# A replaced table of order keys, an earlier bias row, and five weight subtractions moved to GpSimd, in a fused attention and mixture-of-experts kernel

## The chip, the cores and the metric

One core of a Trainium2 chip. The metric is the device time of one execution in microseconds (us). The engines are called as in the profile: PE is TensorE (matmuls; PEld its weight loads), DVE is VectorE, ACT is ScalarE, POOL is GpSimd, SP is the engine that issues most DMAs.

## What is computed

```python
# attention: q, k, v (4, 8, 576, 64), s (4, 8, 576)
scores = (1 / sqrt(D)) * np.matmul(q, k.transpose(0, 1, 3, 2))
cum = np.cumsum(np.maximum(s, 0.0), axis=-1)
bias = -(cum[:, :, :, None] - cum[:, :, None, :])
scores = np.where(causal, -1000000000.0, scores + np.minimum(bias, 0.0))
scores = scores - np.max(scores, axis=-1, keepdims=True)
attn = np.exp(scores)
attn = attn / (np.sum(attn, axis=-1, keepdims=True) + 1e-09)
x = np.matmul(attn, v)                      # as 2304 tokens of 512
# first mixture: w1, w2, w3 (512, 768), w_out (768, 512)
h = np.maximum(np.maximum(x @ w1, x @ w2), x @ w3)
x = h @ w_out
# second: 8 experts, one per token
logits = x @ w_gate + modality_bias[modality_id]
e_idx = np.argmax(logits, axis=1)
gate_w = softmax(logits)[np.arange(N), e_idx]
h = np.maximum(x[mask] @ w1[e], 0.0)        # for each expert e, mask = e_idx == e
out[mask] = gate_w[mask, None] * (h @ w2[e])
```

## The kernel before

Attention runs in 16 pairs of heads (32 heads, h = 0 to 31). To keep float32 precision at the matmul's reduced format, operands are split into a rounded high part and a low part (value minus high). Per head, `load_x` brings q and k (L358, L359), `load_k` the two bias rows that are appended to k (L373 for the first pair, from a scratch tile; L375 for the others, from a copy in memory that `rows_out`, L379, writes in two transfers). `k_high` and `q_high` (L387, L390, mostly ACT) round, `k_again` (L393, POOL) rounds k once more beside the bias rows, `k_low` and `q_low` (L397, L400, POOL) subtract. `scores` makes a bank of scores with two matmuls, L407 (high by high) and L408 (low parts and bias rows). Six banks make one causal head, of 288, 448, 288, 320, 192 and 64 columns. On DVE `least` (L416) masks a bank and takes the row's extreme, on ACT `expo` (L423) exponentiates and sums. PE transposes the result (`turn`, L428), DVE or ACT copies it out (`turned`, L433), and once for each pair `values_of` (L463) multiplies with v in 24 matmuls. The sums go through L437 (ACT), L440 (DVE), L444 (PE), L448 (ACT) and two DMAs to be multiplied in at L469 and L473 (DVE).

Between attention's work PE does **fills**: matmuls of the first mixture on batches whose attention is done. `fill` does three matmuls of 128x288 (L249 high by high, L250 and L251 with a low part); 12 matmuls fill a bank, which ACT copies (L502) or DVE folds in by a maximum (L504). `fx_high` (L487, ACT) and `fx_low` (L491, POOL) split the tokens. The same lines L249 to L251 with 128x384 are the rest of the first mixture, after attention.

The weights arrive as float64 and are **converted** in steps on a 128x512 piece: load (L213, SP, 0.5 MB), L225 (ACT), L227, L229, L231 (DVE), a rounding (L234, a DMA by POOL, for nine early pieces; L236, ACT, for fifteen later ones), and the subtraction for the low part, L238 (POOL for the early ones, DVE for the later).

What sets the order: in attention, every step is a `Job` with an engine, an estimated duration, predecessors and a key. `planned` (L117 on) is a list scheduler: on the engine whose next job can start first it takes, among those that can start within 60 ns, the one with the lowest key. A key is the head's number times `KEY["T"]` plus the entry of table `KEY` (L94) for that kind of step. The jobs are then written out in that order and keep it. Behind them come the later conversions (`convert_rest`, L847), 15 in all, six of which are asked for (`LEAD`) before the first projection, and the rest of both mixtures; their order is set by the framework's own scheduler.

Of the kernel before, what the change touches and what calls it, by code (L numbers as in the profile page):

```python
# [5 lines left out]
F32 = mybir.dt.float32  # L6
# [3 lines left out]
ALU = mybir.AluOpType  # L10
# [6 lines left out]
T = B * S  # L17
# [44 lines left out]
LEAD = 6  # L62
# [28 lines left out]
CONV = [(0, 3), (1, 3), (2, 5), (3, 7), (4, 7), (5, 9), (6, 13), (7, 15), (8, 17)]  # L91
W_READY, SET_H = 15000, 24
WIRE_FROM, WIRE_TO, WIRE_SLOW = 1300, 900, 1.0
KEY = {"s3": 262888, "T": 15750, "wl": 29386, "wz": 48740, "w1": 225687, "wd": 68498, "ws": 411529, "lx": 95995, "lv": 209700, "ck": 138477, "kb": -116340, "kl": -53033, "ql": -58361, "s": 115494, "mn": -5610, "ex": 153024, "ds": 361, "t": 18694, "dt": 19213, "cp": -53151, "r1": -208485, "r2": -212716, "rt": 15596, "rc": -242689, "rw": 44183, "pv": -165391, "x": -56845, "xc": 100720, "xs": -74110, "fe": -88191}  # L94
R_MOE1 = (2, 4, 7)
R_MOE2 = (1, 3, 5)

# [84 lines left out]
def fused_kernel(tc, qk, vd, sd, w64, mod, wg, wgt, mb, we, cst, csi, out):  # L182
    nc = tc.nc
    V, A, G, P, SP = nc.vector, nc.scalar, nc.gpsimd, nc.tensor, nc.sync
    top = ExitStack()
    with top:
# [33 lines left out]
        def converted(f, k, pool, tag, raw, early):  # L220
            h = pool.tile([128, 512], F32R, tag=tag, name="w_h")
            lo = pool.tile([128, 512], F32R, tag=tag, name="w_l")
            z = zsp.tile([128, 512], F32, name="w_z")
            zi = z.bitcast(I32)
            A.activation(out=z, in_=raw.bitcast(F32)[:, :, 1], func=ACTF.Abs, scale=2.0 ** -112)  # L225
            yield
            V.tensor_scalar(out=zi, in0=zi, scalar1=3, scalar2=None, op0=ALU.logical_shift_left)  # L227
            yield
            V.scalar_tensor_tensor(out=zi, in0=raw[:, :, 0], scalar=29, in1=zi, op0=ALU.logical_shift_right, op1=ALU.bitwise_or)  # L229
            yield  # L230
            V.scalar_tensor_tensor(out=zi, in0=raw[:, :, 1], scalar=-2 ** 31, in1=zi, op0=ALU.bitwise_and, op1=ALU.bitwise_or)  # L231
            yield
            if early and W_DMA:
                G.dma_start(out=h, in_=z)  # L234
            else:
                A.copy(out=h, in_=z)  # L236
            yield
            (G if early else V).tensor_tensor(out=lo, in0=z, in1=h.bitcast(F32), op=ALU.subtract)  # L238
            W[f][0][k] = h
            W[f][1][k] = lo  # L240

# [18 lines left out]
        with ExitStack() as es:  # L260

            s3 = xbp.tile([32, 3, S], F32, tag="xb", name="s3")
# [83 lines left out]
            def job(name, run, eng, ns, key, **k):  # L346
                j = Job(run, eng, ns, key, **k)
                jobs.append(j)
                st[name] = j
                return j  # L350

            def at(h, what, n=0):
                return h * KEY["T"] + KEY[what] + n

            def load_x(h):
                p, j = divmod(h, 2)
                x = tl["x", h] = qkp.tile([128, 2, S], F32, name="qk_r", bufs=QR_BUFS)
                SP.dma_start(out=x[64:128, 1], in_=qk[PORD[p], 64:128, 1, j])  # L358
                (SP if h else A).dma_start(out=x[:, 0], in_=qk[PORD[p], :, 0, j])  # L359
                if h == 0:  # L360
                    SP.dma_start(out=mask[:, S - 128:S], in_=cst[:, 256:384])
                    SP.dma_start(out=ident, in_=cst[:, 0:128])

            def k_tile(h):
                if ("k_b", h) not in tl:
                    tl["k_b", h] = qkp.tile([66, S], F32R, name="k_b", bufs=KB_BUFS)
                return tl["k_b", h]

            def load_k(h):
                p, j = divmod(h, 2)  # L370
                k_b = k_tile(h)
                if p == 0:
                    SP.dma_start(out=k_b.bitcast(F32)[64:66], in_=augk.bitcast(F32)[16 * j + PORD[0]:16 * j + PORD[0] + 1])  # L373
                else:
                    SP.dma_start(out=k_b.bitcast(F32)[64:66], in_=dk[PORD[p], :, j])  # L375
# [5 lines left out]
            def values_in(p):  # L381
                v_r = tl["v_r", p] = vp.tile([128, 5, 128], F32, name="v_r")
                SP.dma_start(out=v_r, in_=vd[PORD[p]])

            def k_high(h):
                hl = tl["hl", h] = qkp.tile([128, 2, S], F32R, name="hl", bufs=HL_BUFS)
                (G.tensor_copy if h in CK_POOL else A.copy)(out=hl[64:128, 0], in_=tl["x", h][64:128, 1])  # L387
# [4 lines left out]
            def k_again(h):  # L392
                G.tensor_copy(out=k_tile(h)[0:64], in_=tl["x", h][64:128, 1])  # L393

            def k_low(h):
                hl = tl["hl", h]
                (V if h in KL_DVE else G).tensor_tensor(out=hl[0:64, 0], in0=tl["x", h][64:128, 1], in1=hl.bitcast(F32)[64:128, 0], op=ALU.subtract)  # L397

            def q_low(h):
                G.tensor_tensor(out=qbs[h % QB_N][0:64], in0=tl["x", h][0:64, 0], in1=tl["hl", h].bitcast(F32)[0:64, 1], op=ALU.subtract)  # L400
# [17 lines left out]
            def expo(h, c):  # L418
                p, j = divmod(h, 2)
                if ("l", p) not in tl:  # L420
                    tl["l", p] = ss.tile([128, 2, 5], F32, name="l")
                ec = e_bufs[h % E_N][:, EOFF[c]:EOFF[c] + QC[c][2]]
                A.activation(out=ec, in_=ec, func=ACTF.Exp, bias=tl["mn", h][:, c:c + 1], scale=-1.0, accum_out=tl["l", p][:, j, c:c + 1])  # L423
# [54 lines left out]
            def w_step(n, k):  # L478
                if k == 0:
                    tl["conv", n] = converted(*tl["raw", n])  # L480
                next(tl["conv", n], None)
# [27 lines left out]
            for n, h in CONV:  # L509
                raw, z = Slot("raw"), Slot("z")  # L510
# [4 lines left out]
            sums_s = a = job("s2", s_sums, "DVE", 1346, -1e9, after=[a])  # L515
            b = job("s3", s_high, "ACT", 575, KEY["s3"], after=[a], ready=4350)
            a = job("s4", s_from, "DVE", 360, -1e9, after=[a], lock=True)
            s_low_ = job("s5", s_low, "DVE", 750, -1e9, after=[a, b], lock=True)
            rows = job("rows", rows_out, "SP", 1300, -1e8, after=[s_low_], wire=300)
            turns, highs = None, []  # L520
            for h in range(2 * NP):
                p, j = divmod(h, 2)
                s_x, s_k, s_h, s_q, s_e = (Slot(n) for n in ("qk", "kb", "hl", "qb", "e"))
                lx = job(("lx", h), lambda h=h: load_x(h), "SP", 1900 if h == 0 else 1130, at(h, "lx") if h > 2 else -1e9 + h, takes=[s_x], ready=750, wire=1700)
                if j == 0:
                    s_v, s_p, done = Slot("vr"), [], []
                    lv = job(("lv", p), lambda p=p: values_in(p), "SP", 430, at(h, "lv") if p else -9e8, takes=[s_v], wire=1300, ready=2000)
                ck = job(("ck", h), lambda h=h: k_high(h), "POOL" if h in CK_POOL else "ACT", 671 if h in CK_POOL else 640, at(h, "ck"), after=[lx], takes=[s_h], uses=[s_x], ready=4350)
                cq = job(("cq", h), lambda h=h: q_high(h), "ACT", 600, at(h, "ck", 1), after=[lx, ck], uses=[s_x, s_h])
                if h > 1:  # L530
                    lk = job(("lk", h), lambda h=h: load_k(h), "SP", 300 if h > 1 else 450, at(h, "lx", 1) if h > 1 else -2e8 + h, after=[rows], takes=[s_k], wire=100)
                kb = job(("kb", h), lambda h=h: k_again(h), "POOL", 657, at(h, "kb"), after=[lx, lk] if h > 1 else [lx], takes=[s_k] if h < 2 else [], uses=[s_x, s_k])
                if h < 2:
                    lk = job(("lk", h), lambda h=h: load_k(h), "SP", 300 if h > 1 else 450, at(h, "lx", 1) if h > 1 else -2e8 + h, after=[kb, s_low_], uses=[s_k], wire=100)
                kl = job(("kl", h), lambda h=h: k_low(h), "DVE" if h in KL_DVE else "POOL", 850 if h in KL_DVE else 1415, at(h, "kl"), after=[ck], uses=[s_x, s_h], lock=h in KL_DVE, tail=10 if h in KL_DVE else 0)
                ql = job(("ql", h), lambda h=h: q_low(h), "POOL", 1410, at(h, "ql"), after=[cq], takes=[s_q], uses=[s_x, s_h])
                ex = {}
                for n, (c, k) in enumerate(C_ORDER):
# [3 lines left out]
                    if k or c < 4:  # L542
                        ex[c] = job(("ex", h, c), lambda h=h, c=c: expo(h, c), "ACT", EXP_NS[c], at(h, "ex", n * KEY["ds"]), after=[a], uses=[s_e], tail=0)
                done += ex.values()
# [298 lines left out]
        rest = [(f, k) for f in range(NPRE, NF1) for k in range(3)] + [(f, 3) for f in range(NF1)]  # L843

        N_REST = len(rest)
# [9 lines left out]
        early = []  # L855
        late = []
        for w in range(NW):
# [25 lines left out]
            for i in range(MW // 128):  # L883
                t = w * (MW // 128) + i
# [82 lines left out]
        at = unp.tile([128, U + 1], F32, name="at")  # L967
# [98 lines left out]
```

## Time and profile before

| | before |
|---|---|
| runs, lowest / median / highest | 733.42 / 734.62 / 736.40 us |
| the profiled execution | 734.0 us |
| its span, first to last instruction | 732.2 us |
| busy, share of the span: PE / DVE / ACT / POOL | 97% / 68% / 55% / 31% |
| DMA, mean over the span | 142 GB/s |
| granted TensorE clock, mean | 0.999 |

The span is the time from the first to the last instruction; the execution's own time has 1.8 us more around it. A share of busy time is an average over stages with different limits, so the stretches are looked at one by one below.

### The profile page before, as it was taken

Reading aid. Unit: us, or ns where it says so; the run is one execution under the profiler, and the core shown is the slowest. Engines: PE = TensorE matmul, PEld = TensorE weight load, DVE = VectorE, ACT = ScalarE, POOL = GpSimd, SP = SyncE. Lnnn points to the kernel's source line nnn. Section 1 sums busy time; section 2 is a strip of 40 time slices with the busy share of each in tenths; the row PEclk is TensorE's granted clock in tenths of the full one; section 3 lists DMA queues with packets and bytes.
Section 4 is the critical chain, followed back from the end, with each engine's and each line's share of the span. In section 5 each row is a group of like instructions: output and inputs, shape, how many; then the busy total and the mean of one; then the engine's idle time right before and its main releaser. Section 6 shows DMA issues by size and latency. Waiting matters only on the chain. (4 is left out here: it accounts for less than half of the span.)

```text
span 732.2 us, 13634 instructions
## 1 busy us (share of the span) xinstructions
PE 708.2 (97%) x4602; PEld 633.5 (87%) x4602; DVE 497.4 (68%) x1542; ACT 399.9 (55%) x984; POOL 225.3 (31%) x235
## 2 busy tenths in 40 slices
PE   4899999999999999999999999999999999999996
PEld 3677788878899899899999898999889988999884
DVE  5999787978667932673959796747775665565640
ACT  6899989898644511222222322636564765566631
POOL 8789868776101300010010101041421222212101
PEclk9999999999999999999999999999999999999999
DMA  7476666655236400101001101767567666666600
GB/s 214 144 219 188 203 184 212 190 151 147 81 127 209 164 26 6 49 1 31 36 23 54 52 21 51 258 159 247 153 214 265 225 208 220 212 224 226 222 35 19
DMA packets 43535, 103.83 MB, mean 142 GB/s; under 512 B 9472, under 2 KB 13472, under 8 KB 43456
## 3 DMA queue, kind: packets, MB, share of 16 engines
q1 hardware_dynamic: 35808, 86.04, 37.6%
q0 software_dynamic: 4912, 11.82, 5.1%
q10 hardware_dynamic: 2736, 5.01, 1.9%
q8 instruction: 38, 0.62, 0.4%
q14 instruction: 41, 0.34, 0.2%
HBM read 88.83 MB, written 12.18 MB: 138 GB/s over the span
## 5 line engine op out<-in xcount | busy, mean ns | idle before, releaser
L249 PE MATMUL a_ps<-xh,w_h 128*128 128x384 f32 (+2 forms) x492 | 159.4, 325 | 1.9 <-DVE h L504 1.1
L251 PE MATMUL a_ps<-xh,w_l 128*128 128x384 f32 (+2 forms) x492 | 155.8, 318 | 0.0
L250 PE MATMUL a_ps<-xl,w_h 128*128 128x384 f32 (+2 forms) x492 | 155.7, 317 | 0.0
L768 DVE TENSOR_TENSOR e_l<-e_raw,e_h 128x512 fp32r<-128x512 f32 x160 | 103.9, 689 | 13.5 <-ACT e_h L767 12.1
L767 ACT CAST e_h<-e_raw 128x512 fp32r<-128x512 f32 x160 | 92.9, 622 | 15.9 <-DMA e_raw<-in_we 6.9
L249 PEld LDWEIGHTS a_ps<-xh,w_h 128*128 128x128 f32 x492 | 92.6, 188 | 3.8 <-DVE h L504 1.4
L423 ACT ACTIVATE e<-e,mn 128x448 f32<-128x448 f32 (+4 forms) x160 | 88.6, 557 | 8.5 <-DVE mn L416 8.1
L250 PEld LDWEIGHTS a_ps<-xl,w_h 128*128 128x128 f32 x492 | 92.7, 188 | 0.3
L676 POOL DMA_INDIRECT table<-meta,si x18 | 19.6, 1088 | 238.1 <-DVE nm L664 83.2
L251 PEld LDWEIGHTS a_ps<-xh,w_l 128*128 128x128 f32 x492 | 92.4, 188 | 0.1
L798 PE MATMUL h_ps<-x2t,e_h 128*128 128x256 f32 x288 | 81.0, 282 | 0.0
L799 PE MATMUL h_ps<-x2t,e_l 128*128 128x256 f32 x288 | 80.9, 282 | 0.0
L797 PE MATMUL h_ps<-x2t,e_h 128*128 128x256 f32 x288 | 80.5, 282 | 0.0
L651 DVE CUSTOM_DVE_ANT_0 junk<-x,wg 128x512 bf16<-128x512 f32 x96 | 65.8, 686 | 17.2 <-ACT x L729 16.3
L407 PE MATMUL s_ps<-hl 128*128 128x288 f32 (+1 forms) x192 | 66.0, 354 | 9.9 <-DVE hl L397 6.9
L428 PE MATMUL t_ps<-ident,e 128*128 128x128 f32 x480 | 70.1, 280 | 1.4 <-DVE pt L433 0.6
L416 DVE CUSTOM_DVE_ANT_0 e<-s_ps,mask 128x288 f32<-128x288 f32 (+4 forms) x160 | 63.4, 424 | 9.5 <-PE s_ps L408 9.1
L827 PE MATMUL y_ps<-e_h,gh 128*128 128x512 f32 x152 | 61.5, 405 | 0.4 <-ACT gh L819 0.4
L408 PE MATMUL s_ps<-k_b,q_b 66*128 66x288 f32 (+1 forms) x192 | 57.9, 317 | 4.1 <-DMA k_b<-augk 3.9
L428 PEld LDWEIGHTS t_ps<-ident,e 128*128 128x128 f32 x480 | 56.0, 143 | 5.7 <-DVE pt L433 2.0
L829 PE MATMUL y_ps<-e_h,gl 128*128 128x512 f32 x152 | 60.7, 400 | 0.0
L828 PE MATMUL y_ps<-e_l,gh 128*128 128x512 f32 x152 | 60.0, 395 | 0.0
(179 smaller groups left out, 1484.0 us busy)
## 6 DMA issues: line engine op xcount, KB each, us to landing
e_raw<-in_we SPq DMA_DIRECT2D x80, 512.0 KB
w_raw<-in_w SPq DMA_DIRECT2D x24, 512.0 KB
qk_r<-in_qk SPq DMA_DIRECT2D x31, 288.0 KB
v_r<-in_vd SPq DMA_DIRECT2D x16, 320.0 KB
rb<-r_d SPq DMA_DIRECT2D x32, 160.0 KB
qk_r<-in_qk SPq DMA_DIRECT2D x32, 144.0 KB
x2d<-x ACTq DMA_DIRECT2D x18, 256.0 KB
w_h<-w_z POOLq DMA_DIRECT2D x9, 256.0 KB, 3.9
```

The source lines that it names most:

```text
L249: P.matmul(a_ps, wh[:, c], xh, start=c == 0, stop=False)
L250: P.matmul(a_ps, wh[:, c], xl, start=False, stop=False)
L251: P.matmul(a_ps, wl[:, c], xh, start=False, stop=c == 3)
L407: P.matmul(s_ps, hl[:, 1, q0:q0 + 128], hl[:, 0, k0:k0 + n], start=True, stop=False)
L423: A.activation(out=ec, in_=ec, func=ACTF.Exp, bias=tl["mn", h][:, c:c + 1], scale=-1.0, accum_out=tl["l", p][:, j, c:c + 1])
L428: P.transpose(out=t_ps[:, n * 128:(n + 1) * 128], in_=e_bufs[h % E_N][:, EOFF[c] + kb * 128:EOFF[c] + (kb + 1) * 128], identity=ident)
L651: V.tensor_tensor_reduce(out=junk, in0=x2, in1=wg_sb[ei // 2][:, ei % 2, :], scale=1.0, scalar=0.0, op0=ALU.mult, op1=ALU.add, accum_out=l ...
L767: A.copy(out=h, in_=raw[:, a])
L768: V.tensor_tensor(out=lo, in0=raw[:, a], in1=h.bitcast(F32), op=ALU.subtract)
L797: P.matmul(h_ps, w(hs, f, c), xt[:, 0, c], start=c == 0, stop=False)
L798: P.matmul(h_ps, w(hs, f, c), xt[:, 1, c], start=False, stop=False)
L799: P.matmul(h_ps, w(ls, f, c), xt[:, 0, c], start=False, stop=c == 3)
```

## The change

Three edits. The table of keys is replaced by another, so that the whole order of the attention part changes. The planner is told that the write of the bias rows (`rows`) can't start before 8.5 us of its own clock, and that the first two heads' bias rows take 0.7 us longer to land. And of the 15 later conversions, the first five subtract on POOL instead of DVE. No instruction is added or taken away.

```diff
-KEY = {"s3": 262888, "T": 15750, "wl": 29386, "wz": 48740, "w1": 225687, "wd": 68498, "ws": 411529, "lx": 95995, "lv": 209700, "ck": 138477, "kb": -116340, "kl": -53033, "ql": -58361, "s": 115494, "mn": -5610, "ex": 153024, "ds": 361, "t": 18694, "dt": 19213, "cp": -53151, "r1": -208485, "r2": -212716, "rt": 15596, "rc": -242689, "rw": 44183, "pv": -165391, "x": -56845, "xc": 100720, "xs": -74110, "fe": -88191}
+KEY = {"s3": -97664, "T": 7000, "wl": 40053, "wz": -18589, "w1": 32737, "wd": -43995, "ws": 98173, "lx": -66595, "lv": -5637, "ck": -4681, "kb": -52279, "kl": 21128, "ql": 9680, "s": -4267, "mn": -4185, "ex": 13414, "ds": 50, "t": 10767, "dt": 50, "cp": -42063, "r1": -6337, "r2": -61094, "rt": -71579, "rc": 7287, "rw": -3704, "pv": -70498, "x": -40039, "xc": 39659, "xs": -51512, "fe": 6144}
...
-            (G if early else V).tensor_tensor(out=lo, in0=z, in1=h.bitcast(F32), op=ALU.subtract)
+            (G if early or len(rest) > N_REST - LEAD else V).tensor_tensor(out=lo, in0=z, in1=h.bitcast(F32), op=ALU.subtract)
...
-            rows = job("rows", rows_out, "SP", 1300, -1e8, after=[s_low_], wire=300)
+            rows = job("rows", rows_out, "SP", 1300, -1e8, after=[s_low_], wire=300, ready=8500)
...
-                    lk = job(("lk", h), lambda h=h: load_k(h), "SP", 300 if h > 1 else 450, at(h, "lx", 1) if h > 1 else -2e8 + h, after=[kb, s_low_], uses=[s_k], wire=100)
+                    lk = job(("lk", h), lambda h=h: load_k(h), "SP", 300 if h > 1 else 450, at(h, "lx", 1) if h > 1 else -2e8 + h, after=[kb, s_low_], uses=[s_k], wire=100, land=700)
```

Three places of the order. First SP's queue near the start, as the difference of the two orders (k_b's bias rows, dk their copy in memory, w_raw a weight's piece):

```order
-L373 DMA k_b<-augk 2x1x576
+L373 DMA k_b<-augk 2x1x576 x2
 L379 DMA dk<-augk 32x1x576 x2
-L373 DMA k_b<-augk 2x1x576
```

The second head's L373 went ahead of the two L379. On POOL near there q's low part of the third head now comes ahead of the second head's low part of k.

Second DVE's order around the pair of L229 of the first two conversions; e_130 is the fourth head's result, e_127 the fifth's, pt a copied bank of transposes. Before:

```order
L227 TENSOR_SCALAR w_z<-w_z 128x512
L416 ISA e_130,mn<-s_ps,mask 128x448
L416 ISA mn 128x1
L229 SCALAR_TENSOR_TENSOR w_z<-w_raw,w_z 128x512 x2
L433 COPY pt<-t_ps 128x448
L416 ISA e_130,mn<-s_ps,mask,mn 128x288
L416 ISA mn 128x1
L416 ISA e_130,mn<-s_ps,mask 128x320
```

And in the changed kernel:

```order
L416 ISA e_130,mn<-s_ps,mask 128x320
L416 ISA mn 128x1
L416 ISA e_130,mn<-s_ps,mask 128x192
L416 ISA mn 128x1
L227 TENSOR_SCALAR w_z<-w_z 128x512
L229 SCALAR_TENSOR_TENSOR w_z<-w_raw,w_z 128x512 x2
L416 ISA e_130,mn<-s_ps,mask 128x64
L416 ISA mn 128x1
L416 ISA e_127,mn<-s_ps,mask 128x288
```

The pair moved from behind the head's 448-column bank to behind its 192-column bank, three banks on. In PE's order the first value product (L463) stands just ahead of that head's last bank of 64 columns, L407 and L408. Seven heads of scores stand ahead of the second value product, where six stood.

Third POOL's order at the end of attention (x_1283 and x_2043 are two batches' tokens, q_b the low part of q), in the changed kernel:

```order
L400 TENSOR_TENSOR q_b_125<-qk_r,hl 64x576
L491 TENSOR_TENSOR xl<-x_1283,xh 128x288 x4
L238 TENSOR_TENSOR w_l<-w_z,w_h 128x512 x5
L491 TENSOR_TENSOR xl<-x_1283,xh 128x288 x2
L491 TENSOR_TENSOR xl<-x_2043,xh 128x288 x8
```

The five L238 are the moved subtractions, between the L491; before, none stood there. Counts in PE's order say what became of the fills: of 506 matmuls of 288 columns, 114 stood ahead of the twelfth pair's value product and 213 ahead of the sixteenth's; now 78 and 156. Ahead of the second pair's there are none in either. On SP, of the weight loads behind attention, one that was third among them is now fifth.

## Rows read from the trace of the kernel before

**Rows 1.** The page's busy totals: busy us (share of span) xinstructions.

```profile
PE 708.2 (97%) x4602; PEld 633.5 (87%) x4602; DVE 497.4 (68%) x1542; ACT 399.9 (55%) x984; POOL 225.3 (31%) x235
```

**Rows 2.** PE's waits: what waited for whom, us in total, times, longest us.

```profile
PE s_ps L407 <- DVE hl L397: 6.9, 1, 6.9
PE s_ps L408 <- DMA k_b<-augk: 3.9, 1, 3.9
PE s_ps L407 <- DVE mn L416: 2.6, 3, 1.4
PE a_ps L249 <- DVE h L504: 1.1, 1, 1.1
```

**Rows 3.** Windows: length, then PE, PEld, DVE, ACT, POOL busy, PEclk, DMA, GB/s.

```profile
41.40:158.90 117.50, 116.17 (x906) 95.98 (x904) 99.43 (x344) 110.66 (x320) 94.14 (x86) 1.00 0.69 199
158.90:209.90 51.00, 49.86 (x387) 41.80 (x385) 34.63 (x119) 37.85 (x113) 20.37 (x19) 1.00 0.34 96
209.90:250.00 40.10, 38.30 (x266) 36.05 (x263) 34.05 (x61) 19.29 (x37) 7.78 (x8) 1.00 0.62 203
```

**Rows 4.** Timeline of the start: start us, us, engine, line, operation, [idle before].

```profile
8.04 0.75 SPq L373 DMA_DIRECT2D k_b<-augk  x1
...
10.69 1.39 POOL L397 TENSOR_TENSOR hl<-qk_r,hl 64x576 fp32r<-64x576 f32 x1
...
11.42 0.58 PE L408 MATMUL s_ps<-k_b,q_b 66*128 66x288 f32 x1 [3.89 <-DMA k_b<-augk]
...
14.44 0.58 PE L407 MATMUL s_ps<-hl 128*128 128x288 f32 x1
```

**Rows 5.** Timeline around the pair of L229, 25 to 32 us.

```profile
25.54 2.81 PE L463 MATMUL o_ps<-pt,v_r 128*64 128x512 f32 x20
...
26.38 3.30 POOL L397 TENSOR_TENSOR hl<-qk_r,hl 64x576 fp32r<-64x576 f32 x2
...
27.04 3.20 DVE L229 SCALAR_TENSOR_TENSOR w_z<-w_raw,w_z 128x512 int32<-128x512 int32 x2
...
31.26 0.30 PE L407 MATMUL s_ps<-hl 128*128 128x64 f32 x1 [1.44 <-DVE mn L416]
```

**Rows 6.** Timeline of PE in the fills behind attention.

```profile
213.00 0.30 PE L249 MATMUL a_ps<-xh,w_h 128*128 128x288 f32 x1
...
213.39 0.29 PE L249 MATMUL a_ps<-xh,w_h 128*128 128x288 f32 x1
```

**Rows 7.** ACT's waits from 41 to 159 us.

```profile
ACT e L423 <- DVE mn L416: 1.9, 4, 0.7
ACT pt L433 <- PE t_ps L428: 1.4, 3, 0.6
ACT r_t L448 <- PE t_ps L444: 1.0, 2, 0.5
ACT w_z L225 <- POOL w_l L238: 0.8, 1, 0.8
```

**Rows 8.** Timeline behind attention, then groups of L504 and L238 (last: min/median/max ns).

```profile
218.46 1.58 POOL L491 TENSOR_TENSOR xl<-x,xh 128x288 fp32r<-128x288 f32 x2 [32.17 <-PE a_ps L251]
...
242.70 4.18 POOL L491 TENSOR_TENSOR xl<-x,xh 128x288 fp32r<-128x288 f32 x4 [20.35 <-ACT xh L487]
...
243.98 1.29 DVE L231 SCALAR_TENSOR_TENSOR w_z<-w_raw,w_z 128x512 int32<-128x512 int32 x1
...
245.70 0.40 PE L249 MATMUL a_ps<-xh,w_h 128*128 128x288 f32 x1 [1.12 <-DVE h L504]
...
250.58 0.68 DVE L231 SCALAR_TENSOR_TENSOR w_z<-w_raw,w_z 128x512 int32<-128x512 int32 x1
...
L504 DVE TENSOR_TENSOR h<-a_ps,h 128x288 f32<-128x288 f32 x28 | 12.7, 454 | 12.4 <-PE a_ps L251 11.8 <-DMA v_r<-in_vd 0.4
...
L238 POOL TENSOR_TENSOR w_l<-w_z,w_h x9: 1272/1279/1614, 40.2 to 159.0; 128x512 fp32r<-128x512 f32 x9
```

## The prediction

> **What bounds the kernel now.** I read the page's busy totals first: TensorE (PE) works 708.2 us of a span of 732.2 [rows 1], so only 732.2 − 708.2 = 24.0 us can be won by order, and the same 24.0 us can grow. The change leaves every instruction's count as it was, so PE's work stays, and the forecast is a sum over changes of PE's idle time. Next the list of what PE waited for [rows 2]: two waits at the start (6.9 us for the first low part of k, 3.9 us for the first bias row) are nearly half of it; the rest is small change, 2.6 us for DVE's minimum (L416) the largest. Then the windows [rows 3], from which the reader is to see who drives each stretch. From 41.4 us (the second pair's value product, L463) to 158.9 (the twelfth pair's) PE works 116.17 of 117.50 us, but ACT is at 110.66: two engines are nearly full, and PE is kept full by fills (L249 to L251 at 128x288), MoE work that is ready while attention waits for ACT and DVE. From 158.9 to 209.9 (the last pair's product) ACT has 51.00 − 37.85 = 13.15 us to spare and PE alone bounds. From 209.9 to 250 PE has only MoE work and still loses 40.10 − 38.30 = 1.80 us.
>
> **The change, part by part.** The profiled execution took 734.0 us, 0.62 below the median of the runs (734.62). The sum is made against 734.0.
>
> *Bias rows in front.* The second head's row (L373) now goes out ahead of the two L379 transfers. The first head's row was already first in its queue at 8.04 us, and PE's first L408 waits for that one until 11.42. The second head's scores began at 14.44, with no wait for theirs [rows 4]. Cost 0: the 3.9 us hang on the first row, which is not moved. On POOL the low part of the third head's q now stands ahead of the second head's low part of k. That one ended at 10.69 + 1.39 = 12.08; put back by one such piece (1.39) it ends at 13.47, still 0.97 us before PE asks at 14.44 [rows 4]. Cost 0; if the cover were gone, up to 0.5. The L379 rows stand one issue of under 1 us later; L375 readers of the third head come us later still. Cost 0.
>
> *The pair of L229 on DVE.* Now two conversion steps (3.20 us together, stretched because two L397 of POOL run beside them) stand ahead of the copy that PE's next bank needs, and PE's L407 at 31.26 had waited 1.44 us on L416 [rows 5]. After the change the pair stands behind the fourth head's 192-column bank, and PE's order there has the first value product, 2.81 us [rows 5], then seven heads of scores before the second product instead of six. So most of the 3.20 us is covered, but by then DVE and ACT have been asked for one head more. Bounds: −1.44 if the wait goes and nothing follows it; +1.4 if the same pair stalls the bank behind it. I take −0.5, a third of what the wait was, because the L416 behind the pair again serves PE at once.
>
> *Fills moved behind attention.* Counted in PE's order, 213 fills of 288 columns stood ahead of the last value product, now 156. Consecutive L249 start 0.39 us apart with two matmuls between [rows 6], so one takes 0.13 us and 57 take 57 × 0.13 = 7.4 us. That work is not lost: it comes behind the last product. The change breaks even on it if the last product comes 7.4 us earlier. Between the second and the twelfth product 36 of them leave (114 to 78, 36 × 0.13 = 4.7 us), so this stretch would have to last 117.5 − 4.7 = 112.8 us, with ACT busy for 110.66 of it: 2.1 us idle instead of 6.84. What ACT waited for there [rows 7]: 1.4 + 1.0 us on PE (banks of transposes), which go with a less loaded PE; 1.9 on L416, of which I let half go, since the extra head in front gives DVE's minima a lead and DVE is at 99.43 of 117.50 [rows 3]; 0.8 on POOL's conversions, which stays. So ACT can give 1.4 + 1.0 + 1.0 = 3.4 us of the 4.7, and PE idles 1.3 us more. Bounds: −1.3 (PE's own 1.33 us of idle in that stretch goes too) and +4.7 (ACT keeps its pace). **Term: +1.3.** From the twelfth to the last product 21 fills leave, and one head of scores has gone to the front; ACT has 13.15 us to spare there, so PE stays the bound. Its 51.00 − 49.86 = 1.14 us of idle may halve: −0.5 (bounds −1.1 and +1).
>
> *Behind attention.* The 1.80 us of idle are waits for the copies and maxima of filled banks; the longest, 1.12 us at 245.70, came behind an L231 of 1.29 us [rows 8]. DVE does conversions without a pause there. Now five L238 leave DVE (5 × 0.68, the length of the same kind of operation when alone [rows 8], = 3.4 us), about three more maxima of 0.45 [rows 8] come in with the 57 fills (−1.4), and PE reaches the same banks 7.4 us later after the last product. DVE's lead over PE so grows by about 9 us, where 1.12 was short. **Term: −1.8**, all of it; bounds −1.8 and +2. On POOL the five L238 are queued between two groups of L491, whose next users are fills that PE reaches us later, so I cost them 0. Of the weight loads (L213) one is asked fifth instead of third, behind two of 0.5 MB, which at 203 GB/s [rows 3] are 2.6 us each, 5.2 together; the same 7.4 us cover it. If that cover fails, PE waits about 2 us, the upper bound.
>
> A row speaks against the move to GpSimd. An L231 beside four L491 took 1.29 us instead of 0.68, and the four took 4.18, 1.05 each, where two of them took 1.58, 0.79 each [rows 8]. So DVE loses 0.6 us per two-input operation that meets POOL, and POOL 0.26: both go on, slower. At five meetings that is 5 × 0.6 = 3.0 of the 3.4 us won, and DVE's gain falls to 0.4; the lead from the later fills remains, so the term stays.
>
> [...]
>
> Sum: −0.5 + 1.3 − 0.5 − 1.8 = −1.5, so 734.0 − 1.5 = **732.5 us**. Within about 0.5% (3.7 us) a measurement of this kernel can't tell a difference, so this is no change.
>
> **The rivals.** *Packed* (faster): ACT gives all 4.7 us and PE's scattered waits go as well: −1.44 at the start pair, −1.3 in the middle, −1.1 in the last pairs, −1.8 behind, together −5.6: 728.4 us. For it: two engines at 94 to 99% were packed once already, and the extra head in front is a buffer. Against: ACT must then work 110.66 of 111.5 us, 99%.
>
> *ACT's pace* (slower): ACT keeps its 6.84 us of idle, PE runs out of fills and waits for it, +4.7 in the middle. The lead that DVE gets behind attention shrinks to what ACT leaves (7.4 − 4.7 = 2.7), so the longest wait, 1.12, may stay and only 1.80 − 1.12 = 0.7 us go: 734.0 + 4.7 − 0.7 = 738.0; with the upper bounds of the start (+1.4) and the last pairs (+1) 740.4. It decides from the point at which ACT's idle in that stretch stays over 2.1 us by more than 3 us; it is slower by over 0.5% from 738.3 on. For it: PE's waits on L416 show that the banks come just in time now. Against: half of ACT's waits are PE's doing.
>
> *Nothing moves*: the bias rows and the later subtractions lie off the path, and the order's gains and losses cancel: 734.0.
>
> [...]
>
> **How the numbers follow.** Forecast 0.45, packed 0.22, ACT's pace 0.20, nothing moves 0.08, GpSimd 0.05. Measured against the median, faster by over 0.5% is below 734.6 − 3.7 = 730.9: all of packed, and 0.08 from the forecast's lower end (start and middle terms nearer their lower bounds): 0.30. Slower is above 738.3: 0.14 of ACT's pace, 0.04 from upper bounds of the others: 0.18. The rest, 0.52, is no change. The range leaves out the outer parts of packed and of ACT's pace, a tenth on each side: 728.5 to 739.
>
> **What would show it.** In the profile after: PE's waits at the start unchanged (6.9 and 3.9 us); no wait of 1.4 us near 31 us; the last value product at about 209.9 − 7.4 + 1.3 − 1.0 = 202.8 us; ACT's idle from the second to the twelfth product near 3.4 us; no wait of PE on L502 or L504 behind the last product. ACT's idle of 6 us or more there and a last product at 206 or later would make the forecast wrong on the slow side; PE's idle under 20 us in all, on the fast side.

## The result, and the profile after

The changed kernel took **740.32 us** in the median of 7 runs (737.53 to 743.17), the kernel before 736.4 in the median of 7 (733.42 to 738.41). The ratio is **1.0057 [1.0035, 1.0079]**: slower by 0.57%, where 732.5 and no change were forecast, and outside the range of 728.5 to 739. The profiled execution took 740.32 us with a span of 738.2, against 734.0 and 732.2, so 6.0 us of span are to be found. The granted clock of TensorE differs between executions of one kernel: its mean over an execution was 0.999 in the profile of before and 0.994 over that kernel's runs beside the experiments below, 0.991 in the profile of after and 0.993 over its 7 runs.

The page of after, busy totals and granted clock in 40 slices; the first line answers to [rows 1]:

```profile
PE 711.8 (96%) x4602; PEld 637.0 (86%) x4602; DVE 501.5 (68%) x1537; ACT 399.5 (54%) x984; POOL 235.5 (32%) x240
...
PEclk9899999999999999999999999999999999999999
```

The counts say that the work is the same (five instructions went from DVE to POOL). PE's busy time has still grown by 711.8 − 708.2 = **3.6 us**. Its idle time went from 24.0 to 738.2 − 711.8 = 26.4, **2.4 us** more. Together they are the 6.0 us.

What PE waited for in after, in the columns of [rows 2]:

```profile
PE s_ps L407 <- DVE hl L397: 7.0, 1, 7.0
PE s_ps L408 <- DMA k_b<-augk: 2.9, 1, 2.9
PE s_ps L407 <- DVE mn L416: 2.2, 6, 0.6
PE t_ps L428 <- ACT pt L433: 1.9, 2, 1.4
PE a_ps L249 <- ACT h L502: 1.7, 1, 1.7
PE a_ps L250 <- POOL xl L491: 1.5, 1, 1.5
PE a_ps L249 <- DVE h L504: 1.0, 1, 1.0
```

The second wait is 1.0 us shorter than before; the last three lie behind attention and come to 4.2 us, where 1.8 were lost in all. Of the fourth, PE's waits for ACT's copies of transposes, 1.4 us lie between the second and the twelfth product; the profile of before has none there for ACT's copies.

Windows of after, in the columns of [rows 3]: from the second to the twelfth value product, to the sixteenth, to 260 us, to the end; then two short stretches of a low clock; last the start.

```profile
43.01:159.51 116.50, 112.91 (x872) 91.58 (x870) 105.90 (x350) 110.66 (x322) 100.82 (x88) 1.00 0.72 204
159.51:204.44 44.93, 44.40 (x358) 37.37 (x356) 30.64 (x101) 32.98 (x99) 14.98 (x17) 1.00 0.29 86
204.44:260.00 55.56, 51.23 (x353) 48.86 (x350) 39.77 (x67) 22.98 (x45) 15.15 (x13) 0.97 0.49 161
260.00:738.20 478.20, 471.69 (x2856) 432.19 (x2854) 292.80 (x914) 198.38 (x430) 69.02 (x68) 1.00 0.37 124
33.00:39.20 6.20, 6.14 (x27) 5.93 (x28) 5.23 (x21) 5.09 (x17) 5.93 (x7) 0.50 0.58 163
236.80:241.40 4.60, 4.60 (x24) 4.60 (x25) 4.25 (x10) 1.97 (x3) 0.00 (x0) 0.63 0.73 250
0.00:43.01 43.01, 31.55 (x172) 27.01 (x174) 32.35 (x108) 34.52 (x93) 35.52 (x57) 0.92 0.64 185
```

The same of before where [rows 3] has no such stretch:

```profile
209.90:260.00 50.10, 48.30 (x342) 46.03 (x339) 40.31 (x72) 22.60 (x44) 9.37 (x10) 1.00 0.54 179
0.00:41.44 41.44, 28.14 (x166) 23.44 (x168) 31.01 (x100) 31.32 (x84) 33.38 (x55) 1.00 0.63 181
260.00:732.20 472.20, 465.75 (x2810) 426.27 (x2808) 292.09 (x911) 197.53 (x427) 68.10 (x66) 1.00 0.38 125
```

Length less PE's busy time gives PE's idle time by stretch:

| stretch | before | after | change | forecast |
|---|---|---|---|---|
| start to second product | 13.30 | 11.46 | −1.84 | −0.5 |
| second to twelfth | 1.33 | 3.59 | +2.26 | +1.3 |
| twelfth to sixteenth | 1.14 | 0.53 | −0.61 | −0.5 |
| sixteenth to 260 us | 1.80 | 4.33 | **+2.53** | **−1.8** |
| 260 us to the end | 6.45 | 6.51 | +0.06 | 0 |
| sum | 24.0 | 26.4 | +2.4 | −1.5 |

The last product came at 204.44 us: 5.4 us earlier than before, where the 57 moved fills needed 7.4.

How far do such figures repeat? e1 and e4 below have the same new order. Their idle times in the three middle rows are 3.45 and 3.50, 0.53 in both, and 3.79 and 4.40 us; e3, whose order is that of before but for one transfer, has 1.31, 1.14 and 1.65. The start repeats less well: 12.64 and 11.63 in e1 and e4, where the program up to there is that of after, and 14.22 and 13.78 in e2 and e5, where it is that of before.

The clock. After ran at 0.50 from 32.8 to 39.6 us, behind two short pauses of PE (the third in the rows below comes when the clock has fallen), and again from 237.6 to 241.0, behind the pauses of 1.05 and 1.74 us shown below. The profile of before shows neither: 1.00 from 33 to 39 us and from 237 to 241 (in the last 2.2 us both fall, to a mean of 0.50 in after and 0.69 in before). e1 has both falls too, with a mean of 0.66 from 30 to 40 us and 0.87 from 230 to 240; e4 has one early on, of 3.4 us (0.83 from 30 to 40), and none near 237 (1.00 from 230 to 250), though PE waited 2.5 us there; before, e2, e3 and e5, of the old order, have 1.00 there. In the second stretch the fills show it: groups of three matmuls stand 0.72 us apart, where they stood 0.39 apart in [rows 6]. Timeline of after, PE:

```profile
30.59 0.41 PE L407 MATMUL s_ps<-hl 128*128 128x288 f32 x1 [0.54 <-DVE mn L416]
32.05 0.36 PE L407 MATMUL s_ps<-hl 128*128 128x192 f32 x1 [0.52 <-DVE mn L416]
33.06 0.58 PE L407 MATMUL s_ps<-hl 128*128 128x288 f32 x1 [0.16 <-DVE mn L416]
...
237.57 0.45 PE L249 MATMUL a_ps<-xh,w_h 128*128 128x288 f32 x1
238.29 0.45 PE L249 MATMUL a_ps<-xh,w_h 128*128 128x288 f32 x1
```

Now the pauses behind attention. Timeline of after, all engines, 229 to 254 us:

```profile
229.60 4.12 POOL L491 TENSOR_TENSOR xl<-x,xh 128x288 fp32r<-128x288 f32 x4 [5.18 <-ACT xh L487]
...
229.78 1.30 DVE L238 TENSOR_TENSOR w_l<-w_z,w_h 128x512 fp32r<-128x512 f32 x1
...
231.50 0.40 PE L249 MATMUL a_ps<-xh,w_h 128*128 128x288 f32 x1 [1.05 <-DVE h L504]
...
231.92 1.13 DVE L238 TENSOR_TENSOR w_l<-w_z,w_h 128x512 fp32r<-128x512 f32 x1
...
232.97 1.03 DVE L227 TENSOR_SCALAR w_z<-w_z 128x512 int32<-128x512 int32 x1
...
235.71 0.62 ACT L236 CAST w_h<-w_z 128x512 fp32r<-128x512 f32 x1 [1.96 <-DVE w_z L231]
236.23 0.39 ACT L502 COPY h<-a_ps 128x288 f32<-128x288 f32 x1
236.68 0.40 PE L249 MATMUL a_ps<-xh,w_h 128*128 128x288 f32 x1 [1.74 <-ACT h L502]
...
253.56 0.40 PE L250 MATMUL a_ps<-xl,w_h 128*128 128x288 f32 x1 [1.45 <-POOL xl L491]
```

Read the three rows from 235.71 to 236.68 backwards. PE waits 1.74 us for ACT's copy L502 of a full bank. That copy, 0.39 us long, stands in ACT's queue behind the rounding L236 of a weight's conversion, and L236 had waited 1.96 us for DVE's L231. Before that, three of DVE's steps ran long beside POOL's four L491: the two L238 1.30 and 1.13 instead of 0.68, L227 1.03 instead of 0.42, 1.7 us together. So the copy was late for no reason of its own: it was queued behind a conversion.

### The profile page after: what moved, and what is told of

The parts are those of the page before. It is cut to its first block, busy times and chain, and to the rows that moved or that the text cites. A ratio compares the mean times of both kernels' runs of the same rounds, so it can differ in the third digit from the quotient of the medians.

```text
span 738.2 us, 13662 instructions
## 1 busy us (share of the span) xinstructions
PE 711.8 (96%) x4602; PEld 637.0 (86%) x4602; DVE 501.5 (68%) x1537; ACT 399.5 (54%) x984; POOL 235.5 (32%) x240
## 5 line engine op out<-in xcount | busy, mean ns | idle before, releaser
L407 PE MATMUL s_ps<-hl 128*128 128x288 f32 (+1 forms) x192 | 66.1, 355 | 9.2 <-DVE hl L397 7.0
L416 DVE CUSTOM_DVE_ANT_0 e<-s_ps,mask 128x288 f32<-128x288 f32 (+4 forms) x160 | 62.8, 420 | 4.8 <-PE s_ps L408 4.7
L408 PE MATMUL s_ps<-k_b,q_b 66*128 66x288 f32 (+1 forms) x192 | 58.8, 322 | 2.9 <-DMA k_b<-augk 2.9
```

The source lines that it names most:

```text
L407: P.matmul(s_ps, hl[:, 1, q0:q0 + 128], hl[:, 0, k0:k0 + n], start=True, stop=False)
```

## The experiments

Ten kernels ran. Those named together shared their runs of the kernel before, whose medians were 735.29 us (e1 to e4), 736.77 (e5 to e7) and 735.08 (e8 to e10).

**e1: the changed order, the five subtractions back on DVE.**

```diff
-(G if early or len(rest) > N_REST - LEAD else V).tensor_tensor(out=lo, ...)
+(G if early else V).tensor_tensor(out=lo, ...)
```

> The changed kernel with its five L238 back on VectorE; the new table and the bias row in front stay, and the third load behind attention (w_raw 3775) stands third again. Theory A (the moved subtractions cost the time, behind attention): the last value product stays near 204.4 us, PE's waits behind it fall from 4.2 us to 1.8 or less, the clock does not fall there; span near 734, ratio to the kernel before 1.000 to 1.003. Theory B (the new attention order costs it): waits behind stay above 3 us in some form and the span stays near 738, ratio 1.005 or more.

Measured 739.88 us, ratio 1.0057 [1.0038, 1.0077], the same as the whole change. PE's waits in e1, 205 to 260 us:

```profile
PE a_ps L249 <- ACT h L502: 2.4, 1, 2.4
PE a_ps L250 <- POOL xl L491: 1.3, 1, 1.3
```

3.7 us behind attention, not 1.8 or less. The theory that the subtractions on GpSimd cost the time falls: in this order they are worth nothing that these intervals show, and the weight load, which is third again in e1, isn't it either. In e1 too POOL's four L491 (229.64 to 234.02) stand just ahead of the long pause, which ends at 236.78.

**e2: the kernel before with only the five subtractions on POOL.**

```diff
-(G if early else V).tensor_tensor(out=lo, ...)
+(G if early or len(rest) > N_REST - LEAD else V).tensor_tensor(out=lo, ...)
```

> The kernel before with nothing changed but the five L238 on GpSimd (attention's order unchanged; the load of w_raw 3775 moves from third to fifth here too). Theory A: waits of PE behind the last product (209.9 us) rise from 1.8 us to about 4, span up by 2 to 4.5 us, ratio 1.003 to 1.006. Theory B: nothing beyond noise, ratio within 0.998 to 1.002, waits near 1.8.

Measured 737.94 us, ratio 1.0035 [1.0021, 1.0049]. PE's waits behind attention in e2:

```profile
PE a_ps L249 <- DVE h L504: 1.6, 3, 1.0
PE a_ps L250 <- POOL xl L491: 0.9, 1, 0.9
```

2.5 us where 1.8 stood before. In the old order the move does cost, about a third of a per cent, 2.6 us. The profile places only 1.0 us of it behind attention (2.75 us of idle instead of 1.80). It also has a fall of the clock (0.66 from 30 to 40 us) and 0.9 us more idle at the start, where the program is that of before; so most of the 2.6 us isn't located. The move doesn't add visibly to what the new order costs.

**e3: the kernel before with only the second bias row ahead of the two L379.**

```diff
+sequence.insert(sequence.index(st["rows"]), sequence.pop(sequence.index(st["lk", 1])))
```

> The kernel before with the second head's L373 ahead of the two L379 and no other instruction moved. If the first bias row lands late because the L379 transfers share the way with it (theory C): the first L408 starts at about 10.45 us instead of 11.42, its wait falls from 3.9 to 2.9 us, and the span falls by 0 to 1 us. If the first row's landing does not depend on what follows it in the queue (my prediction's step): 11.42 and 3.9 as before.

Measured 735.2 us, ratio 0.9989 [0.9972, 1.0007]. The wait at the start, in e3:

```profile
PE s_ps L408 <- DMA k_b<-augk: 2.7, 1, 2.7
```

2.7 us instead of the 3.9 of [rows 2], and the second product came at 40.23 instead of 41.44, so theory C, that the first row lands earlier, holds. The gain, about 1 us in the profile, is too small for the interval to exclude no change. Among the runs whose mean clock was 0.999 it does show: four of e3 took 732.57 to 733.19 us, five of before 733.81 to 734.38.

**e4: the changed kernel with only the first of the five subtractions on POOL.** The weight load stays fifth here.

```diff
-(G if early or len(rest) > N_REST - LEAD else V).tensor_tensor(out=lo, ...)
+(G if early or len(rest) >= N_REST - 1 else V).tensor_tensor(out=lo, ...)
```

> The changed kernel with only the first of the five L238 on GpSimd; w_raw 3775 stays the fifth load. If the late load carries the cost behind attention: ACT's first wait of L225 for w_raw stays near 3 us, PE's waits behind the last product stay near 4 us, span near 738. If the share of GpSimd's own slower subtractions carries it (five of 1.28 us, their hold on the two w_z buffers, the L491 behind them): waits near 2 us, span 734 to 735.

Measured 740.69 us, ratio 1.0079 [1.0057, 1.0100]. PE waited 2.5 us on L502 and 1.8 on L491. That is roughly what the first alternative forecast, but e1, whose load is third again, loses as much. One, five or no subtraction on POOL: the loss is the same within the intervals.

**e5: the kernel before with its last 19 groups of fills (57 matmuls) moved behind the last value product**, and with them the splits, copies and maxima that stand among them; nothing else of the order changes. The edit, written out line by line:

```diff
+pv = sequence.index(st["pv", NP - 1])
+fills = [n for n, j in enumerate(sequence[:pv]) if j.name[0] == "f"]
+late = [j for j in sequence[fills[-19]:pv] if j.name[0] in ("f", "fe", "fo", "xc", "xs")]
+sequence = [j for j in sequence[:pv + 1] if j not in late] + late + sequence[pv + 1:]
```

> The kernel before, its table and its VectorE subtractions kept; of the fills that its order has ahead of the last value product the last 19 triples (57 matmuls of 288 columns, 7.4 us of PE) are taken out and put right behind that product, with the steps that feed and drain them. Theory D (what lies behind attention can't take 57 more fills: they need more low parts from GpSimd and more copies by ScalarE and maxima by VectorE while the late conversions run there): the last value product comes some 6 to 7 us earlier, near 203 us, but PE's waits behind it rise from 1.8 us to 4 or more, and the ratio to the kernel before is 1.002 to 1.005. My prediction's step (the extra fills give VectorE a lead and the waits go): waits under 1 us, ratio 0.997 to 0.999. If the attention order alone costs the time: ratio 1.000, waits as before.

Measured 741.6 us, ratio 1.0069 [1.0051, 1.0087]. Windows of e5, as above:

```profile
42.62:160.05 117.43, 116.09 (x906) 95.90 (x904) 97.95 (x344) 110.75 (x320) 94.30 (x85) 1.00 0.68 196
160.05:208.22 48.17, 43.96 (x330) 34.14 (x328) 32.63 (x115) 36.52 (x110) 20.39 (x19) 1.00 0.35 98
208.22:260.00 51.78, 48.98 (x338) 45.36 (x335) 41.01 (x71) 22.24 (x43) 8.96 (x8) 1.00 0.52 172
```

57 matmuls left the second row's stretch. PE's busy time there fell by 49.86 − 43.96 = 5.9 us, less than the 7.4 of the prediction's 0.13 us each, and the stretch became only 51.00 − 48.17 = 2.8 us shorter: PE idles 4.21 us there instead of 1.14, 2.3 of them in six waits for ACT's copies of transposes. Behind the product it idles 2.80 instead of 1.80. Theory D had the product near 203 us and waits of 4 us or more behind it: the product came at 208.22, and the waits were 2.7. Late fills alone thus cost on both sides, more ahead of the product than behind it. Unlike the change, e5 takes all 57 out of the last four pairs. The changed plan does the first half better (0.53 us idle, with 21 fills gone and the others taken elsewhere) and the second half worse.

**e6: e3 with the pair of L229 moved** to where the change has it, behind the fourth head's 192-column bank. **e9: e3 with only the second of the two moved.**

```diff
+two = [[j for j in sequence if j.name == ("w", n)][2] for n in (0, 1)]
+sequence = [j for j in sequence if j not in two]
+at_ = sequence.index(st["mn", 3, 1, 0]) + 1
+sequence = sequence[:at_] + two + sequence[at_:]
```

> The kernel before with two moves at the start and nothing else: the second head's L373 ahead of the two L379, and on VectorE the pair of L229 behind the fourth head's 192-column bank instead of behind its 448-column bank. If the pair's place is what makes PE wait at 31 us: the wait of 1.44 us on L416 there goes to under 0.7, the second value product comes 1 to 2 us earlier than 41.4, and with fewer pauses there the granted clock falls less often near 33 us: mean clock of the runs above 0.996, ratio 0.995 to 0.998. If the pair only moves the wait to the next bank: a wait of over 1 us on L416 within 30 to 36 us, second product at 40.2 as with the moved row alone, ratio 0.998 to 1.000.

> The kernel before with the second head's L373 ahead of the two L379, and of the pair of L229 on VectorE only the second moved, behind the fourth head's 192-column bank. If one L229 of about 1.6 us at each place is short enough for PE's banks: each wait on L416 between 28 and 34 us is under 0.8 us, mean clock of the runs 0.996 or more, ratio to the kernel before 0.996 to 0.998. If both places now make PE wait and the granted clock falls near 33 us as in the runs with the pair moved: mean clock 0.993 to 0.994, ratio 0.999 to 1.002.

Measured 737.18 us, ratio 1.0017 [1.0001, 1.0033], and 736.52 us, 1.0010 [0.9997, 1.0023]. Timeline of e6, PE:

```profile
32.83 0.61 PE L407 MATMUL s_ps<-hl 128*128 128x288 f32 x1 [1.69 <-DVE mn L416]
```

The wait of 1.44 us at 31.26 [rows 5] didn't go; it is 1.69 at 32.83, at the bank behind the pair's new place. In e9 the longest is 1.5. Both are no faster than e3, and e6 is slower than before by just more than its interval.

**e10: e3 with three late conversions asked for ahead of the first projection instead of six.**

```diff
-LEAD = 6
+LEAD = 3
```

> The kernel before with the second head's L373 ahead of the two L379, and three instead of six late conversions asked for ahead of the first projection, which lets drains of filled banks stand between fewer conversion steps. If the place of the drains among the conversion steps sets PE's pauses behind attention: the waits on L502 and L504 behind the last product fall from 1.6 us to under 0.5 and the ratio is 0.996 to 0.998. If the weights then come too late for PE: a new wait on w_h or w_l of over 1 us, ratio 1.000 or more.

Measured 735.79 us, ratio 1.0008 [0.9994, 1.0023]. The waits behind attention come to 1.6 us (0.9 on L491, 0.7 on L504), as in e3: how many conversions are asked for ahead moves them from one line to another and doesn't set their sum.

**e7: e1 without the 15 late subtractions. e8: e7 also without the late conversions' three other steps on DVE.** Both leave parts of the computation out, so their total times say nothing here; they are read up to 300 us.

```diff
-(G if early else V).tensor_tensor(out=lo, ...)
+early and G.tensor_tensor(out=lo, ...)
...
-W[f][1][k] = lo
+W[f][1][k] = lo if early else h
...
-V.tensor_scalar(out=zi, ...)
+early and V.tensor_scalar(out=zi, ...)
```

The third pair of lines, and the same for both `scalar_tensor_tensor`, is e8's alone.

> The changed kernel with its subtractions on VectorE, and the fifteen late conversions leave their subtraction (L238) out; the low part of those weights is then the high part again, so the values behind, and the routing to experts, differ, and only the stretch to 300 us is compared. If PE's waits on L502 and L504 behind attention come from the chain of conversion steps that stands ahead of them on ScalarE and VectorE: the wait of 2.4 us on L502 goes to under 1 us; the wait on the low parts from GpSimd (L491, 1.3 us near 252 us) stays. If they come from elsewhere (loads of raw weights, late low parts): the wait on L502 stays above 2 us.

> The changed kernel with the fifteen late conversions stripped of every step on VectorE (L227, L229, L231 and the subtraction L238 left out); loads, the two ScalarE steps and everything else stay. The weights' values and the routing differ, so only the stretch to 300 us is compared. If PE's pauses behind attention come from drains of filled banks (L502, L504) that stand behind conversion steps on VectorE and ScalarE, and from low parts that VectorE's steps slow down: PE's waits on L502, L504 and L491 behind the last product fall from 3.7 us (subtractions on VectorE) and 2.5 us (no subtractions) to under 1 us. If they come from the raw loads or from the fills' own feed: still 2 us or more.

PE's waits behind attention in e7:

```profile
PE a_ps L249 <- ACT h L502: 1.2, 1, 1.2
PE a_ps L249 <- DVE h L504: 1.1, 2, 0.9
```

With 0.2 on L491 they are 2.5 us, down from 3.7: less than expected, and the wait on L491 didn't stay as expected. The window of e8 from its last value product to 260 us:

```profile
205.31:260.00 54.69, 54.60 (x392) 52.31 (x389) 9.09 (x20) 22.46 (x47) 7.85 (x10) 1.00 0.47 167
```

PE works 54.60 of 54.69 us at a clock of 1.00. ACT still does all its copies and roundings (22.46 us), DVE its maxima, POOL its low parts, and the raw weights still arrive; only DVE's conversion steps are gone. So the pauses behind attention hang on those steps. Three things go with them, and no run takes them apart: the drains that stood behind them on DVE, ACT's waits for them (L236 and L225, with the copies L502 behind), and what they and POOL's L491 cost each other (four L491 in a row took 3.11 us in e8, 4.12 in after, where DVE's L238 beside them took 1.30 instead of 0.68). Each of the long pauses of before (ending at 245.70), after and e1 comes during four L491 in a row or within 3 us behind them.

## Why the prediction was wrong

**The step that failed: *Behind attention*, "Term: −1.8, all of it".** It was +2.53 us of idle, 4.3 away and past its upper bound of +2, more than the whole difference between the forecast's sum (−1.5) and the measured idle (+2.4). The argument was that PE reaches the same banks 7.4 us later, so DVE's lead grows by about 9. That treats DVE as a stock of finished work that waits for PE, and it rests on "DVE does conversions without a pause there", which [rows 3] don't give: DVE is at 34.05 of 40.10 us. The time that was to become a lead became idle time: in the windows up to 260 us DVE idles 50.10 − 40.31 = 9.79 us before and 55.56 − 39.77 = 15.79 after. DVE's conversions didn't run ahead: part of that idle time are their waits for ACT, and ACT waited for the raw weights. Both waits grew. Before:

```profile
DVE w_z L227 <- ACT w_z L225: 2.9, 4, 2.3
ACT w_z L225 <- DMA w_raw<-in_w: 3.5, 3, 2.3
```

And after:

```profile
DVE w_z L227 <- ACT w_z L225: 6.2, 4, 2.5
ACT w_z L225 <- DMA w_raw<-in_w: 5.2, 3, 3.1
```

Drains (L502, L504) and low parts (L491) can't run ahead either: each waits for PE's bank or for ACT's split, and then stands in a queue in program order between conversion steps, as the copy at 236.23 stood behind the rounding at 235.71. How late the conversions end depends on where the five subtractions run, but the loss doesn't. ACT's last L225 of that stretch, before:

```profile
250.69 0.69 ACT L225 ACTIVATE w_z<-w_raw 128x512 f32<-128x512 f32 x1 [1.28 <-DVE w_l L238]
```

After, with five subtractions on POOL, and then in e1, with none there:

```profile
250.72 0.68 ACT L225 ACTIVATE w_z<-w_raw 128x512 f32<-128x512 f32 x1
...
246.85 0.69 ACT L225 ACTIVATE w_z<-w_raw 128x512 f32<-128x512 f32 x1
```

In e1 the conversions end 3.8 us earlier than before, attention 5.0, and PE still idles 3.79 us.

So 57 fills more, which before were drained inside attention, are drained among conversions. e8 shows that the pauses hang on the conversion steps (no steps on DVE, 0.09 us of idle). e5 shows that late fills are enough for some of the rise (1.0 us), and e1 and e4 rule out the subtractions and the late load, which the prediction had held against this term. How much of the 2.53 is due to the number of fills, how much to the new places of the drains among the conversions, and how much to where POOL's four L491 fall was not separated; that part of the cause is argued, not shown. The pauses of 1.05 and 1.74 us come 95 and 119 matmuls of 288 columns behind the last product, so they are not at the first 57 themselves.

**"PE's work stays" failed too**: its instructions stayed, its time grew by 3.6 us, at the clock of 0.50. At 0.50 from 32.8 to 39.6 us and from 237.6 to 241.0 at most half of 6.8 + 3.4, 5.1 us, is lost. But this part must not be put down to the change alone. The profile of before was an execution with no fall, 0.999, and 734.0 us; in a later series of 23 runs of that kernel (beside e8 to e10) the four at 0.999 took 733.0 to 733.8 us and the three at 0.990 735.6 to 737.2. The runs of before had a mean of 0.994 beside the experiments, those of after 0.993. By that series (3.2 us for 0.009) a difference of 0.001 to 0.002 is about 0.5 us of the medians' 3.9. Nor is the clock most of it: the three runs of after with a mean of 0.996 or 0.997 took 737.53 to 740.36 us, while no run of before beside the experiments with 0.994 to 0.996 took more than 736.33. The prediction leaned on an execution at the quick end of its kernel's runs: the forecast of 732.5 was 1.5 under that one, and 3.9 under the later median.

**Second to twelfth product**: right in kind, +2.26 against +1.3 and inside its bounds. 36 fills left, ACT stayed at 110.66 us of work, and of its 6.84 us of idle it gave 1.00 (116.50 − 110.66 = 5.84), where I had 3.4. So here the rival *ACT's pace* was nearer: its own condition, idle of ACT over 2.1 us by more than 3, was met with 3.7, and its 738.0 to 740.4 holds the result. But it had the time lost in this stretch and 0.7 us won behind attention, where more was lost than here; so that its figure fits is in part luck. The prediction's own signs of being wrong on the slow side, ACT's idle of 6 us or more and a last product at 206 or later, did not come (5.84 and 204.44). No experiment changes this stretch by itself.

**Twelfth to sixteenth**: −0.61 against −0.5, right, though e5 shows that it isn't the mere absence of fills that gives it.

**Bias rows, "Cost 0: the 3.9 us hang on the first row, which is not moved"**: wrong by 1.0 us, in the good direction. Timeline of after (SPq is SP's queue):

```profile
8.05 1.41 SPq L373 DMA_DIRECT2D k_b<-augk  x2
...
9.50 1.30 SPq L379 DMA_DIRECT2D dk<-augk  x2
...
10.45 0.58 PE L408 MATMUL s_ps<-k_b,q_b 66*128 66x288 f32 x1 [2.92 <-DMA k_b<-augk]
```

The first row is issued when it was (8.04 in [rows 4]), and PE has it at 10.45 instead of 11.42. What changed is only what is issued behind it: e3 shows the same with nothing else changed (a wait of 2.7 us instead of 3.9).

**The pair of L229, −0.5**: not supported. In after the one wait of 1.44 became three of 1.22 us together; in e6, by itself, the wait moved on to the next bank, and in e9, with one of the two moved, PE waited at both places (1.16 and 1.52 us). Beside POOL's subtractions the pair took 3.20 us in before and 3.12 in e6; the median of one L229 in before is 0.69. Of the −1.84 at the start only the row's 1 us or so is clear of the spread between executions of the same program there (11.46 to 12.64 in after, e1 and e4).

**GpSimd** (0.05 of the chances): moving the subtractions cost time where it stands alone (e2, ratio 1.0035), and none that shows in the changed order (e1). Each engine took longer beside the other: in after DVE's L238 took 1.30 us instead of 0.68 beside four L491 of 1.03 each, which took 0.79 each at 218.46 in [rows 8]. Beside the moved subtractions DVE lost unequal amounts: its L688 at 210.45 took 1.55 us beside a POOL L238 of 1.29 (0.55 in e1), its L238 at 223.95 took 1.01 beside one of 1.75, and its L231 at 222.57, beside the same one, no more than 0.69. So the prediction's 0.6 us for each meeting was an estimate from one. The prediction's "both go on, slower" says more than its rows do: the 0.6 us that DVE loses is less than one L491 alone (0.79), so waiting for the rest of one would look the same.

What stays open: why the clock falls at 33 us in some executions and not in others, what the new order does to the stretch from the second to the twelfth product in detail, and some 1 us of the 3.9 between the medians, which is within the ratio's interval (2.6 to 5.8 us).

## What to carry to other kernels

Before filler work is moved behind a stage, list what drains it there, engine by engine in program order: a copy of 0.4 us behind a step that itself waits is as late as that step (here the L502 of 0.39 us behind an L236 that had waited 1.96), and a lead on paper doesn't help a drain that can't start before its bank is full. Take the idle time of each stretch apart from the engine's busy time, and look at the granted clock of several executions (0.990 to 0.999 here, for one kernel) before one profile is used as the base of a sum. Of the parts, only the earlier bias row showed a gain, about 1 us at the start, which its interval does not separate from none (0.9989 [0.9972, 1.0007]), and no kernel here beat the one before by more than its interval.

## What the runs showed of the hardware

A small transfer was there for PE about 1 us earlier when two larger ones were issued behind its neighbour instead of directly behind it, though its own issue time was the same (8.04 us in before, 8.05 in after). PE used it at 10.45 in after, against 11.42 in before; PE's wait for it was 2.7 us in e3 and 2.9 in after, against 3.9 in before and 3.7 in e5. In e2, which has the order of before, that wait was 3.1, but behind a wait for L397 of 7.8 instead of 6.9: the two come to 10.9 us, and to 10.8 in before. The mechanism is open.

The clock fell to 0.50 behind PE's short pauses at 30 to 33 us in some executions and not in others, and pause length alone didn't tell which: a longest wait on L416 of 1.4 us (before, e3) and 1.5 (e10) went without a fall, at a mean clock of 0.999 in all three; in after the fall at 32.8 us came behind waits of 0.54 and 0.52, and e9, whose longest was 1.5 too, had a mean of 0.994. In e2 and e5 that part of the program is the same as before, and their longest wait was 2.3, with means of 0.993 and 0.994 (in e2 0.66 from 30 to 40 us).

DVE's L227, which reads only one tensor, took longer beside GpSimd too: 1.03 us instead of 0.42 at 232.97 in after, while POOL ran its four L491 (229.60 to 233.72); in e1 it was again 1.03, at 232.32, beside the four there.
